# New charges for five kinds of elementwise work in a build-time plan, and a new table that steers it

## The chip, the core and the metric

The kernel runs on one core of one Trainium2 chip. The metric is the device time of one launch in microseconds (us); the time before is 1015.88 us, the median of three runs (1014.32 to 1016.97). A core has five engines that run side by side, each with its own queue of instructions: TensorE (PE in the profile, with its weight loads as PEld) multiplies matrices into eight banks of PSUM; VectorE (DVE), ScalarE (ACT) and GpSimd (POOL) do elementwise work; SyncE (SP) issues the transfers, which sixteen DMA engines carry out. An instruction that needs another engine's result waits for it at the head of its own queue, and everything behind it waits too.

## The reference

Two attention blocks, A and B, read the same x (2048 tokens of 640 numbers) with their own weights, and a gate per token mixes their outputs. One block projects x to q, k and v, splits them into 32 heads of 20 and the tokens into 4 segments of 512. For each segment and head it takes causal softmax attention inside the segment and reads a memory M, z that holds the segments before:

```python
logits = einsum("bhqd,bhkd->bhqk", qs, ks) * scale + mask
a_dot  = einsum("bhqk,bhkd->bhqd", softmax(logits), vs)
pq  = phi(qs)                      # t + 1 where t > 0, else exp(t)
a_mem = einsum("bhld,bhde->bhle", pq, M) / (einsum("bhld,bhd->bhl", pq, z) + 1e-6)
o   = g * a_mem + (1.0 - g) * a_dot     # g = sigmoid(beta), one per head
M, z = M + phi(ks)^T vs, z + sum(phi(ks))
```

The block's output is o times wo, and the kernel's is `gate * a + (1 - gate) * b` with `gate = sigmoid(x . gate_w)`.

## The kernel before

The work is cut into eight rows t = 0 to 7: row t is block t % 2 in segment t // 2. A row has jobs for TensorE (projections of q, k, v and, one row later, of the output; 128 rows of the result at a time) and eight quads, each of four heads, so 64 quads in all. A quad i has ten score units (five S, which give the row maxima, and five T, which give the transposed scores for the exponentials) and one unit of attention times v. Between them stand smaller units: transposes, reads of the memory (`mem_unit`) and its updates. Products are made of three terms, since each operand is split into a high part (the rounded copy) and a low part (what rounding left). Most matmuls use half of the array's rows, and two such run side by side.

The order on every queue is written out when the kernel is built. The build runs a plan: a clock, a queue per engine (A, D, G, S for ScalarE, VectorE, GpSimd and SyncE) and a charge in microseconds for every piece of work. `put` (line 200) queues a piece with its charge and adds the charge to the engine's load; when the plan's engine is free, the piece of the best priority is written out, and what depends on it follows after the charge. TensorE's instructions are written out as the plan's clock moves on (`step`, line 1649). So the charges decide when the plan believes that an operand is there, and with it what TensorE's queue holds at that place. They don't delay anything on the chip. Three places choose an engine by load: `anyof` (line 217) takes the one whose load and charge are least in sum, `either` does it for ScalarE and VectorE, and `hi_lo_phi` (line 720) takes one of two ways through the feature map phi.

A table, `RULES`, steers the plan slot by slot (66 slots; one quad's S and T units fall in each; a slot without a row keeps the settings of the one before). `rules` (line 1690) reads eight settings: the order of the S and T units; `span`, the share of the slot over which they are spread; `calm`, the load on VectorE above which units of low priority, the memory's among them, are held back; `lag`, the time between the two halves of a product; `room`, the free buffers that T units need; `hold`, how much earlier a slot begins; `wait` and `wait2`, how long small units are held before they are taken.

The lines of the change lie in the weighing of a row's dots. For rows 0 to 6 the attention's sums go to DRAM (`send_dot`) and come back rearranged. When all eight quads of a row are there, `reciprocals` (line 1377) multiplies the denominators by the gates (line 1379, VectorE) and inverts them in two halves (line 1384). `mix` (line 1404) then handles five tiles of 128x512: the product with the inverse (line 1429 on VectorE or line 1430 on GpSimd), from row 2 on the transposed memory part added by VectorE (line 1496), the high part by ScalarE (line 1420), and the low part (line 1422 on VectorE or line 1423 on GpSimd). The output job of the row waits for them. GpSimd also makes the low parts of weights (line 543) and of x (line 590), and it masks the exponentials (line 1292). VectorE makes the row maxima (line 1196), and with three instructions it closes a memory unit (lines 897, 899 and 900).

Of the kernel before, what the change touches and what calls it, by code (L numbers as in the profile page):

```python
# [16 lines left out]
ALU = mybir.AluOpType  # L17

P = 128
D = 640  # L20
S = 2048
# [3 lines left out]
L = 512  # L25
KT = D // P
NB = L // P
# [10 lines left out]
def r32(ap):  # L38
    return ap.bitcast(F32)
# [3 lines left out]
def tile_gated_mix_infini_attn(  # L43
# [17 lines left out]
    nc = tc.nc  # L61
# [27 lines left out]

    RULES = {  # L90
# [60 lines left out]
    }  # L151
    rule = {}
    DONE = {"A": 0.27, "D": 0.26, "G": 0.22, "S": 0.0}
    FULL, LEADT = 0.113, 0.056
# [45 lines left out]
    def put(e, dur, emit, then=None, prio=5):  # L200
        heapq.heappush(ready[e], (prio, next(seq), dur, emit, then))
        load[e] += dur
        start_next(e)
# [1172 lines left out]

    def reciprocals(t, d, g):
        def gates():
            put("D", 0.9, lambda: nc.vector.scalar_tensor_tensor(
                out=r32(d), in0=r32(d), scalar=gcol[t % 2], in1=r32(g), op0=ALU.mult, op1=ALU.mult), lambda: half(0), prio=2)  # L1380

        def half(c):
            cols = slice(L // 2 * c, L // 2 * (c + 1))
            put("D", 1.78, lambda: nc.vector.reciprocal(r32(d[:, cols]), r32(d[:, cols])),
                (lambda: half(1)) if c == 0 else done, prio=2)
            if c == 0:
                big.give(g)

        def done():
            inverse[t] = d  # L1390
            for fn in waiting.pop(t, []):
                fn()

        landed = then_all(2, gates)
        b = t % 2
        dma(0.8, lambda: nc.sync.dma_start(
            out=r32(d), in_=lanes_of(t)[:, DH:DH + 1, :].to_broadcast([H, 4, L])), landed, prio=-1, lat=1.2)
        dma(0.8, lambda: nc.sync.dma_start(
            out=r32(g), in_=rowg[t // 2][NB * b:NB * b + NB, :].rearrange("n p -> (n p)")[None, :].to_broadcast([P, L])), landed, prio=-1, lat=1.2)
# [4 lines left out]
    def mix(t, k, y):  # L1404
# [14 lines left out]
        def two_parts(hi, lo):  # L1419
            put("A", 0.515, lambda: nc.scalar.copy(hi, r32(y)), lambda: anyof(  # L1420
                2, lambda: (big.give(y), OTs.__setitem__((t, k), (hi, lo))),
                D=(0.85, lambda: nc.vector.tensor_tensor(out=lo, in0=r32(y), in1=r32(hi), op=ALU.subtract)),  # L1422
                G=(1.25, lambda: nc.gpsimd.tensor_tensor(out=lo, in0=r32(y), in1=r32(hi), op=ALU.subtract))), prio=2)

        def weigh():
            r = inverse[t]
            anyof(
                2, weighed,
                D=(0.9, lambda: nc.vector.tensor_tensor(out=r32(y), in0=r32(y), in1=r32(r), op=ALU.mult)),  # L1429
                G=(1.4, lambda: nc.gpsimd.tensor_tensor(out=r32(y), in0=r32(y), in1=r32(r), op=ALU.mult)))  # L1430

        def landed():
            if t in inverse:
# [358 lines left out]
```

## Time and profile before

| | |
|---|---|
| median of three runs | 1015.88 us (1014.32 to 1016.97) |
| profiled execution, its own time | 1016.54 us |
| its span, first to last instruction | 1014.8 us |
| mean granted TensorE clock | 0.995 of full speed |
| busy: TensorE, weight loads | 1002.1 us (99%), 855.5 us (84%) |
| busy: VectorE, ScalarE, GpSimd | 769.3 us (76%), 659.5 us (65%), 612.3 us (60%) |

The page gives busy time per engine. A table of stretches gives the same per window: first the window, then its length, then busy time and number of instructions for TensorE, its weight loads, VectorE, ScalarE and GpSimd, then the granted clock, the share of the DMA engines in use and GB/s. A group's row gives line, engine, operation, what it writes and reads, the shapes and the count, then busy us and mean ns of one, then the engine's idle time before such instructions and who ended it. A timeline's row gives start, length, engine, line and operation, and in brackets the idle time before it and who ended it; rows with a count of more than one are merged. The chain of waits follows the end back to the start; its rows give start, length and what it was.

### The profile page before, as it was taken

The page shows a single profiled execution, that of the slowest core. Times are in us where ns is not written, and L with a number is a line of the kernel's source. Part 1 is how long each engine was busy: PE and PEld are TensorE (multiplying, and loading weights), DVE is VectorE, ACT ScalarE, POOL GpSimd, SP SyncE. Part 2 cuts the span into 40 slices and gives each one's busy share as a digit, 9 for nine tenths or more (in the row PEclk, how much of TensorE's full clock was granted, in tenths as well). Part 3 has the DMA queues.
Part 4 walks back from the last instruction along what each step waited for, and adds up shares of the span by engine and source line. Part 5 has one row for each costly group of instructions (what it writes and reads, how often), then busy time and mean ns, then how long its engine had stood idle before and what let it go on. Part 6 is the DMA issues. An engine that isn't in the chain of part 4 may idle for free.

```text
span 1014.8 us, 30827 instructions
## 1 busy us (share of the span) xinstructions
PE 1002.1 (99%) x11260; PEld 855.5 (84%) x11260; DVE 769.3 (76%) x2604; ACT 659.5 (65%) x1341; POOL 612.3 (60%) x1040
## 2 busy tenths in 40 slices
PE   9999999999999999999999999999999999999998
PEld 7998888888888888878888878897889888878876
DVE  4688777976787778877578976888567897689764
ACT  5376776776566767757766666675676666675672
POOL 4465657676476655775646656486675656567571
PEclk9999999999999999999999999998999999999999
DMA  7999989898896988866768687795876979688531
GB/s 248 308 306 270 298 255 305 274 283 259 262 286 185 286 237 245 268 183 219 237 177 300 188 267 234 206 301 175 252 230 182 313 213 281 206 228 267 151 93 62
DMA packets 148886, 241.99 MB, mean 238 GB/s; under 512 B 13216, under 2 KB 46144, under 8 KB 148416
## 3 DMA queue, kind: packets, MB, share of 16 engines
q1 hardware_dynamic: 148736, 240.03, 77.2%
q8 instruction: 89, 1.46, 0.6%
q14 instruction: 61, 0.50, 0.2%
HBM read 150.83 MB, written 94.65 MB: 242 GB/s over the span
## 4 chain that ended last, share of the span: by engine, by line
PE 84%; DMA 6%; DVE 5%; ACT 1%; POOL 1%; issue 1%; SPq 1%; ACTq 0%; DVEq 0%; POOLq 0%
PE bank L773 50%; PE bank L1319 13%; PE bank L1299 7%; PE bank L1209 7%; PE bank L883 3%; PE bank L965 3%; PE bank L925 2%; DMA row<-dots 1%; DMA dots<-row 1%; DMA kd<-row 1%; DVE bank L1196 1%; PE bank L1234 1%; DVE row L1429 1%; DVE row L1422 1%; DMA row<-in_xT_dram 1%
## 5 line engine op out<-in xcount | busy, mean ns | idle before, releaser
L1196 DVE CUSTOM_DVE_ANT_0 bank<-bank,tri 128x256 f32<-128x256 f32 (+3 forms) x1024 | 474.7, 520 | 150.2 <-PE bank L1209 96.8
L773 PE MATMUL bank<-row,wh 64*128 64x512 f32 x2308 | 498.6, 403 | 0.6 <-DVE mw L897 0.6
L1291 ACT ACTIVATE p<-bank 128x512 f32<-128x512 f32 x588 | 324.0, 601 | 140.0 <-PE bank L1299 108.4
L1292 POOL TENSOR_SCALAR_AFFINE_SELECT p<-p 128x256 f32<-128x256 f32 (+1 forms) x588 | 219.2, 380 | 228.6 <-ACT p L1291 219.2
L773 PEld LDWEIGHTS bank<-row,wh 64*128 64x128 f32 x2308 | 319.8, 186 | 11.8 <-issue 1.1
L773 PE MATMUL bank<-row,wl 64*128 64x512 f32 x1154 | 293.3, 402 | 0.0
L543 POOL TENSOR_TENSOR wl<-wst,wh 128x640 fp32r<-128x640 f32 x115 | 181.3, 1581 | 58.1 <-ACT wh L541 51.7
L1209 PE MATMUL bank<-kst,qst 60*128 60x384 f32 (+3 forms) x1024 | 184.0, 317 | 1.8 <-DVE row L1349 0.8
L773 PEld LDWEIGHTS bank<-row,wl 64*128 64x128 f32 x1154 | 173.6, 186 | 5.0 <-issue 0.6
L1299 PE MATMUL bank<-qst,kst 62*128 62x128 f32 (+3 forms) x1024 | 176.4, 317 | 1.0 <-ACT vst L1015 0.5
L773 PE MATMUL bank<-wvh,row 64*128 64x320 f32 x1280 | 176.7, 312 | 0.0
L1319 PE MATMUL bank<-p,vst 128*32 128x384 f32 (+3 forms) x1936 | 148.9, 431 | 0.0
L773 PEld LDWEIGHTS bank<-wvh,row 64*128 64x128 f32 x1280 | 147.4, 185 | 1.0 <-issue 0.2
L1196 DVE DVE_READ_ACCUMULATOR2_ANT mx<- 128x1 f32 x1024 | 144.6, 141 | 0.0
L1209 PEld LDWEIGHTS bank<-kst,qst 60*128 60x128 f32 x1024 | 137.5, 186 | 8.2 <-DVE row L1349 1.2
L1299 PEld LDWEIGHTS bank<-qst,kst 62*128 62x128 f32 x1024 | 130.5, 186 | 7.3 <-DVE mx L1196 1.0
L1319 PEld LDWEIGHTS bank<-p,vst 128*32 128x32 f32 x1936 | 59.3, 110 | 87.4 <-issue 62.7
L541 ACT CAST wh<-wst 128x640 fp32r<-128x640 f32 x119 | 86.4, 741 | 20.2 <-PE bank L773 14.4
L773 PE MATMUL bank<-wvl,row 64*128 64x320 f32 x640 | 99.3, 310 | 0.0
L1349 ACT COPY row<-bank 128x512 f32<-128x512 f32 x61 | 36.0, 590 | 79.4 <-PE bank L1319 71.1
L773 PEld LDWEIGHTS bank<-wvl,row 64*128 64x128 f32 x640 | 80.0, 185 | 0.6 <-issue 0.4
L518 POOL TENSOR_TENSOR wvl<-wst,wvh 128x640 fp32r<-128x640 f32 (+1 forms) x48 | 64.0, 1338 | 17.3 <-ACT wvh L515 17.3
(117 smaller groups left out, 1213.5 us busy)
## 6 DMA issues: line engine op xcount, KB each, us to landing
qst<-qd SPq DMA_DIRECT2D x128, 240.0 KB
kst<-kd SPq DMA_DIRECT2D x128, 240.0 KB
qd<-row SPq DMA_DIRECT2D x40, 512.0 KB
kd<-row SPq DMA_DIRECT2D x40, 512.0 KB
dots<-row SPq DMA_DIRECT2D x56, 256.0 KB
wst<-wmix SPq DMA_DIRECT2D x35, 320.0 KB
row<-dots SPq DMA_DIRECT2D x42, 256.0 KB
qd<-row SPq DMA_DIRECT2D x40, 256.0 KB
```

What stands on the lines that cost most here:

```text
L518: put("G", 0.77 * n, lambda: nc.gpsimd.tensor_tensor(out=wl[:, a:b, :], in0=w3, in1=r32(wh[:, a:b, :]), op=ALU.subtract), end, prio=4)
L541: put("A", 0.625, lambda: nc.scalar.copy(wh, w3), lambda: put(lo_eng, lo_cost, lambda: lo.tensor_tensor(out=wl, in0=w3, in1=r32(wh), op=AL ...
L543: lambda: lo.tensor_tensor(out=wl, in0=w3, in1=r32(wh), op=ALU.subtract), end, prio=3), prio=6)
L773: return nc.tensor.matmul(bank_of, lhsT=w[ROWS[half]], rhs=x_[ROWS[half]], start=start, stop=stop)
L883: return nc.tensor.matmul(pm[:, a - h0:c - h0, :].rearrange("p h e -> p (h e)"), lhsT=r32(pqTs[t, m][ROWS[half], P * n:P * (n + 1)]), rhs= ...
L1196: put("D", w / 960.0 + 0.105, lambda: nc.vector.tensor_tensor_reduce(out=sc[:, off:off + w], in0=sc[:, off:off + w], in1=tri[:, L - w:], s ...
L1209: lane_ops[half].append((mm(w), lambda pair=pair, qb=qb, off=off, w=w, r=r, sc=sc: nc.tensor.matmul(sc[:, off:off + w], lhsT=q[r, pair, P ...
L1291: put("A", 0.483, lambda: nc.scalar.activation(pt, sc, AF.Exp, scale=SCALE), lambda: (bank.give(sc), put("G", 0.15 + 0.105 * len(todo), la ...
L1292: "G", 0.15 + 0.105 * len(todo), lambda: nc.gpsimd.affine_select(out=blocks, in_=blocks, pattern=[[0, len(todo)], [1, P]], base=0, channel ...
L1299: lane_ops[half].append((mm(w), lambda pair=pair, kb=kb, off=off, w=w, r=r, sc=sc: nc.tensor.matmul(sc[:, off:off + w], lhsT=k[r, pair, P ...
L1319: nc.tensor.matmul(po[32 * j:32 * j + 32, P * kb:], lhsT=vst[t % 2][:, kb, h * E1:h * E1 + 32], rhs=pts[i, n, f][0][:, off:off + w], start ...
L1349: either(0.483, lambda: nc.scalar.copy(r32(oT), po), 0.605, lambda: nc.vector.tensor_copy(r32(oT), po), end, 2)
```

## The change

Five charges change: the gate 0.90 to 1.00, a product on VectorE 0.90 to 1.05 and on GpSimd 1.40 to 1.50, a low part on VectorE 0.85 to 0.95 and on GpSimd 1.25 to 1.35. The table is replaced: row 0 stays, 57 other rows take the place of 59. Counting what a slot without a row inherits, 63 of 66 slots have other settings than before.

```diff
     RULES = {
         0: "TSTSTSTSTS 0.933 2.38 0.30 4 0.0 3.08 1",
-        1: "TSTSTSTSTS 1.010 2.38 0.27 8 0.0 1.6 1.60",
-        2: "TSTSTSTSTS 1.036 2.04 0.30 6 0.0 1.6 0.40",
-        3: "STSTSTSTST 0.976 2.38 0.30 8 0.1 1.6 1",
-        4: "TSTSTSTSTS 1.010 1.52 0.31 8 1.9 1.31 1.66",
...
+        1: "TSTTSSTSTS 0.988 3.22 0.30 4 0.0 1.6 1",
+        2: "STSTSTSTST 0.986 2.38 0.37 8 0.0 1.6 1",
+        3: "TSTSTSTSTS 1.010 1.76 0.35 4 3.4 1.6 1",
+        4: "TSTSTSTSTS 1.029 3.65 0.29 8 0.0 1.6 1",
...
     def reciprocals(t, d, g):
         def gates():
-            put("D", 0.9, lambda: nc.vector.scalar_tensor_tensor(
+            put("D", 1.0, lambda: nc.vector.scalar_tensor_tensor(
...
         def two_parts(hi, lo):
             put("A", 0.515, lambda: nc.scalar.copy(hi, r32(y)), lambda: anyof(
                 2, lambda: (big.give(y), OTs.__setitem__((t, k), (hi, lo))),
-                D=(0.85, lambda: nc.vector.tensor_tensor(out=lo, in0=r32(y), in1=r32(hi), op=ALU.subtract)),
-                G=(1.25, lambda: nc.gpsimd.tensor_tensor(out=lo, in0=r32(y), in1=r32(hi), op=ALU.subtract))), prio=2)
+                D=(0.95, lambda: nc.vector.tensor_tensor(out=lo, in0=r32(y), in1=r32(hi), op=ALU.subtract)),
+                G=(1.35, lambda: nc.gpsimd.tensor_tensor(out=lo, in0=r32(y), in1=r32(hi), op=ALU.subtract))), prio=2)
...
             anyof(
                 2, weighed,
-                D=(0.9, lambda: nc.vector.tensor_tensor(out=r32(y), in0=r32(y), in1=r32(r), op=ALU.mult)),
-                G=(1.4, lambda: nc.gpsimd.tensor_tensor(out=r32(y), in0=r32(y), in1=r32(r), op=ALU.mult)))
+                D=(1.05, lambda: nc.vector.tensor_tensor(out=r32(y), in0=r32(y), in1=r32(r), op=ALU.mult)),
+                G=(1.5, lambda: nc.gpsimd.tensor_tensor(out=r32(y), in0=r32(y), in1=r32(r), op=ALU.mult)))
```

108 rows, old and new, of the table RULES are left out of this document.

## The prediction

> **What bounds the kernel now.** I read the page first, then the table of stretches, then TensorE's timeline around every gap, then the groups of the repriced lines.
>
> ```profile
> span 1014.8 us, 30827 instructions
> PE 1002.1 (99%) x11260; PEld 855.5 (84%) x11260; DVE 769.3 (76%) x2604; ACT 659.5 (65%) x1341; POOL 612.3 (60%) x1040
> ```
>
> TensorE sets the time: 12.7 us of the span are left without a matmul, and some of that is the head and the tail, which the change doesn't touch. In 25 us stretches, these are the inner ones with a visible loss (left out: four that lose under 0.1 us each):
>
> ```profile
> core 0: us, PE busy (x) PEld busy (x) DVE busy (x) ACT busy (x) POOL busy (x), PEclk, DMA share, GB/s
> ...
> 150.00:175.00 25.00, 24.52 (x294) 20.69 (x292) 17.94 (x47) 16.69 (x36) 18.60 (x29) 1.00 0.97 292
> ...
> 300.00:325.00 25.00, 24.23 (x274) 20.26 (x272) 18.92 (x62) 16.02 (x32) 18.87 (x30) 1.00 0.65 193
> ...
> 400.00:425.00 25.00, 24.51 (x301) 21.11 (x293) 21.07 (x57) 16.20 (x34) 17.60 (x28) 1.00 0.90 289
> 425.00:450.00 25.00, 23.35 (x257) 20.32 (x255) 21.25 (x78) 15.45 (x31) 18.40 (x26) 0.93 0.57 174
> ...
> 575.00:600.00 25.00, 24.20 (x270) 21.08 (x268) 20.34 (x74) 15.10 (x31) 14.07 (x33) 1.00 0.86 270
> ...
> 675.00:700.00 25.00, 24.21 (x272) 19.68 (x270) 22.25 (x58) 17.08 (x36) 18.48 (x23) 0.86 0.79 236
> ...
> 925.00:950.00 25.00, 24.49 (x307) 21.35 (x305) 22.42 (x82) 15.66 (x33) 15.94 (x28) 1.00 0.56 165
> ```
>
> Idle in them: 0.48 + 0.77 + 0.49 + 1.65 + 0.80 + 0.79 + 0.51 = 5.49 us. Two also show a lower granted clock: 25 x (1 - 0.93) = 1.75 us and 25 x (1 - 0.86) = 3.50 us, together 5.25 us of lost beats, about as much as the gaps. A new order can win back at most some 10.7 us. The gaps themselves, on TensorE's timeline:
>
> ```profile
> 302.04 0.49 PE L773 MATMUL bank<-row,wh 64*128 64x512 f32 x1 [0.60 <-DVE mw L897]
> 305.98 0.38 PE L1209 MATMUL bank<-kst,qst 60*128 60x256 f32 x1 [0.17 <-DVE O L900]
> 687.72 0.80 PE L1209 MATMUL bank<-kst,qst 60*128 60x512 f32 x2 [0.31 <-DVE row L1496]
> 688.87 0.93 PE L883 MATMUL bank<-mbd,row 64*128 64x84 f32 x3 [0.35 <-ACT p L1291]
> 925.54 0.50 PE L1299 MATMUL bank<-qst,kst 62*128 62x384 f32 x4 [0.33 <-DVE row L729]
> ```
>
> ```profile
> 172.11 0.50 PE L1299 MATMUL bank<-qst,kst 62*128 62x512 f32 x1 [0.48 <-ACT vst L1015]
> 420.91 0.49 PE L1209 MATMUL bank<-kst,qst 60*128 60x512 f32 x1 [0.49 <-ACT row L1349]
> 436.98 0.23 PE L1234 MATMUL bank<-ident,mt 64*32 64x64 f32 x1 [1.59 <-POOL mt L1221]
> 592.18 0.50 PE L1209 MATMUL bank<-kst,qst 60*128 60x384 f32 x4 [0.80 <-DVE row L1349]
> ```
>
> The first fence of gaps (1.76 us) lies where a row's dots are weighed and split, behind VectorE. Its timeline there, with one undisturbed product for comparison:
>
> ```profile
> 185.17 0.69 DVE L1429 TENSOR_TENSOR row<-row,row 128x512 f32<-128x512 f32 x1
> 299.93 1.79 DVE L1422 TENSOR_TENSOR row<-row,row 128x512 fp32r<-128x512 f32 x1
> 302.67 2.44 DVE L1422 TENSOR_TENSOR row<-row,row 128x512 fp32r<-128x512 f32 x2
> 685.14 1.92 DVE L1429 TENSOR_TENSOR row<-row,row 128x512 f32<-128x512 f32 x1
> 919.84 2.86 DVE L1429 TENSOR_TENSOR row<-row,row 128x512 f32<-128x512 f32 x2
> ```
>
> The slow product at 685.14 ran beside this on GpSimd:
>
> ```profile
> 684.98 1.54 POOL L543 TENSOR_TENSOR wl<-wst,wh 128x640 fp32r<-128x640 f32 x1 [0.17 <-ACT wh L541]
> ```
>
> The second fence of gaps (3.36 us) has another cause. ScalarE takes its instructions in their written order and stood behind a transfer:
>
> ```profile
> 170.14 0.62 ACT L586 CAST row<-row 128x512 fp32r<-128x512 f32 x1 [1.19 <-DMA row<-in_xT_dram]
> 417.77 0.62 ACT L586 CAST row<-row 128x512 fp32r<-128x512 f32 x1 [0.68 <-DMA qst<-qd]
> 435.91 0.62 ACT L586 CAST row<-row 128x512 fp32r<-128x512 f32 x1 [2.16 <-DMA row<-in_xT_dram]
> 590.87 0.60 ACT L732 ACTIVATE row<-bank 128x512 f32<-128x512 f32 x1 [2.29 <-DMA kd<-row]
> ```
>
> No edited price bears on these four.
>
> **The change, part by part.** It takes no product, copy or transfer away; it alters charges in the plan and the table that steers it, and so the order on every queue and, where the plan chooses by load, the engine.
>
> ```profile
> L1430 POOL TENSOR_TENSOR row<-row,row 128x512 f32<-128x512 f32 x23 | 31.9, 1406 | 7.1 <-DVE row L1384 5.2 <-DVE fw L1468 1.9
> L1423 POOL TENSOR_TENSOR row<-row,row 128x512 fp32r<-128x512 f32 x19 | 26.5, 1400 | 10.4 <-ACT row L1420 9.7 <-ACT mr L1251 0.6
> L1422 DVE TENSOR_TENSOR row<-row,row 128x512 fp32r<-128x512 f32 x16 | 18.2, 1148 | 0.0
> L1429 DVE TENSOR_TENSOR row<-row,row 128x512 f32<-128x512 f32 x12 | 15.3, 1291 | 0.0
> L1379 DVE SCALAR_TENSOR_TENSOR row<-row,gcol,row 128x512 f32<-128x512 f32 x7 | 7.4, 1053 | 6.7 <-DMA row<-rowg 5.4 <-DMA kst<-kd 1.3
> ```
>
> Prices against means: VectorE's product 0.90 to 1.05 (measured 1.291), its low part 0.85 to 0.95 (1.148), the gate 0.90 to 1.00 (1.053); GpSimd's product 1.40 to 1.50 (1.406), its low part 1.25 to 1.35 (1.400). The undercharge on VectorE was 12 x 0.391 + 16 x 0.298 + 7 x 0.153 = 10.5 us over seven stretches and becomes 12 x 0.241 + 16 x 0.198 + 7 x 0.053 = 6.4 us, so four tenths of the error go. GpSimd goes from 2.9 us short to 23 x 0.094 - 19 x 0.05 = 1.2 us over. The division between the engines should hardly move: for a product the difference of the two prices goes from 0.50 to 0.45, for a low part it stays 0.40. The third choice by load, which of two ways the feature map takes, can shift a pass or two from VectorE to ScalarE:
>
> ```profile
> L722 DVE TENSOR_SCALAR bank<-bank 128x512 f32<-128x512 f32 x35 | 24.3, 701 | 0.0
> L732 ACT ACTIVATE row<-bank 128x512 f32<-128x512 f32 x25 | 15.3, 614 | 3.0 <-DMA kd<-row 2.3 <-DVE row L1422 0.7
> ```
>
> Now 35 tiles go by VectorE and 25 by ScalarE; one more by ScalarE takes 0.70 us off VectorE, and I cost it at nothing, because ScalarE is busy 65% of the span and covers it. Without that cover it would be 0.61 us of ScalarE's time each.
>
> What that buys, gap by gap, is the rise of the charges on the chain just ahead, since the plan then places the waiting matmul that much later and puts other matmuls in front. Before 302.04 stand a product and a low part (0.15 + 0.10 = 0.25 of 0.60). Before 305.98 two low parts (0.20, so all 0.17). Before 687.72 one product (0.15 of 0.31), which the chain of waits shows directly:
>
> ```profile
> 685.28 1.79 DVE row L1429
> 687.07 0.61 DVE row L1496
> ```
>
> I give the 0.35 at 688.87 nothing, since it follows the same delay. Before 925.54 two products (0.30 of 0.33). Sum: 0.25 + 0.17 + 0.15 + 0.30 = 0.87 us. If the table alone decides what stands there, this is 0; if all five gaps go, 1.76.
>
> The larger term is the clock behind 687.72, which stood at half for most of seven microseconds:
>
> ```profile
> 688.00:689.00 1.00, 0.65 (x3) 0.14 (x3) 1.00 (x4) 0.82 (x2) 0.69 (x2) 0.50 0.87 188
> ```
>
> That episode is the 3.50 us of the 675:700 row. I take all of it as won, with ends of 0 and 3.50: longer gaps (0.60 at 302.04, 0.80 at 592.18) dropped no clock, so this needs an unlucky coincidence of a gap with a thin run of short matmuls, and a rewritten stretch will seldom repeat it. [...]
>
> The table gives 63 of the 66 slots other settings (order of score units, spread, load limit, lag, early start, delays), counting what a missing row inherits. No row of the trace prices this. Its ends are one episode like 425:450 lost or gained, 1.65 + 1.75 = 3.40 us each way, and I take the middle, 0: the same transfers, with the same charges in the plan, will be late somewhere. SP's queue is reordered with the rest, so a transfer such as the one of x at 435.91 can as well come earlier as later; who is queued behind a late one is ScalarE's copies, and TensorE behind those. Waits of one half of the array while the other works don't show as idle; they lie in these ends too.
>
> Sum: 1016.54 (the profiled execution: span 1014.8 and 1.74 around it) - 0.87 - 3.50 = 1012.17. That execution lies 0.66 over the median 1015.88 of the runs shown, so the forecast is **1011.5 us**.
>
> **The rivals.** *No change, 1015.0 us.* The crowded stretches keep their stalls, because a flat charge is wrong there both ways: the same product takes 0.69 and 1.92 us, and 0.87 on 1.92 is not covered by 1.05. Only the 0.87 us of gaps go, a half-clock episode comes back somewhere: 1016.54 - 0.87 - 0.66. For it: the new charges are still under the means on VectorE. Against: half-clock episodes number only two in 1,015 us. [...]
>
> *Slower, 1019.3 us.* The load limit ("calm", mostly 2.38 us) holds memory units back while VectorE's queue is charged above it. Three products now add 0.45 us to that queue, so memory units start later, the updates that wait for them too, and with them the values' job of the next row, until TensorE has no unit to fill with. The price is that of the nearest row, 425:450: 1.65 us of gap and 1.75 us of clock, 1015.88 + 3.40. It decides once a memory unit is held longer than the jobs planned between it and the values' job last. For it: VectorE is busy 22.25 of 25 us at 675:700. Against: TensorE waited for a memory bank's reader in only 0.60 + 0.17 us here.
>
> *Much faster, 1005.1 us.* The new order also covers the late transfers: all 5.49 + 5.25 us go, 1015.88 - 10.74 = 1005.1. Against: nothing in the plan's charge for a transfer changes.
>
> **How the numbers follow.** A measurement of this kernel tells 0.3%, 3.05 us, from no change: faster is under 1012.8, slower over 1018.9. Chances: my forecast 0.42 (own range 1008 to 1015), no change 0.23, slower 0.23, much faster 0.12. Faster: 0.32 of my case, 0.12 of the last, 0.01 of no change, 0.45. Same: 0.10 of my case and 0.20 of no change, 0.30. Slower: 0.23 and 0.02 of no change, 0.25. The range reaches from the last case to the slower one with half a further episode (1.75) on it: 1004.5 to 1021.
>
> **What would show it.** Right: VectorE's products and low parts still near 1.2 us each, a 25 us table with at most one stretch of reduced clock, idle in the weighing stretches down to about 1 us, and gaps behind transfers of some 3 us in other places. Wrong: two or more stretches under 0.95 of the clock, or gaps behind the weighing as long as 1.76 us in sum. The forecast fails if the clock episode is not chance but belongs to the weighing, or if the new table moves a late transfer in front of ScalarE's copies more often than four times.

## The result and the profile after

The changed kernel takes 1022.10 us (median of five runs, 1020.31 to 1023.17) where the kernel before, on the same chip, takes 1015.03 us (five runs, 1012.20 to 1016.97). The ratio is 1.007 with an interval of 1.0055 to 1.0085: the change makes the kernel 0.7% slower. The forecast was 1011.5 us in a range of 1004.5 to 1021, so both the sign and the range were wrong.

Lines behind the table stand two lower in the changed kernel: the product of the projections is L771 (it was L773), the weighing's product on VectorE L1427 (L1429), its low part L1420 (L1422). The first lines of the page after:

```profile
span 1020.4 us, 30866 instructions
PE 1005.0 (98%) x11260; PEld 860.1 (84%) x11260; DVE 767.3 (75%) x2592; ACT 665.9 (65%) x1355; POOL 609.7 (60%) x1038
```

The span grew by 5.6 us. TensorE's idle part grew from 12.7 to 1020.4 - 1005.0 = 15.4 us, which is 2.7. The other 2.9 us are *busy* time, 1002.1 to 1005.0, although TensorE runs the same 11260 matmuls, and one by one they lasted as long as before (in the mean 357 ns before, 356 after). Its costliest groups after, with the count, then busy time and the mean ns of one:

```profile
L771 PE MATMUL bank<-row,wh 64*128 64x512 f32 x2308 | 507.5, 404 | 0.0
L771 PE MATMUL bank<-row,wl 64*128 64x512 f32 x1154 | 302.9, 402 | 0.0
L771 PE MATMUL bank<-wvh,row 64*128 64x320 f32 x1280 | 182.3, 314 | 1.7 <-ACT vst L1013 1.7
L771 PE MATMUL bank<-wvl,row 64*128 64x320 f32 x640 | 103.2, 312 | 0.0
```

And the same four of the kernel before:

```profile
L773 PE MATMUL bank<-row,wh 64*128 64x512 f32 x2308 | 498.6, 403 | 0.6 <-DVE mw L897 0.6
L773 PE MATMUL bank<-row,wl 64*128 64x512 f32 x1154 | 293.3, 402 | 0.0
L773 PE MATMUL bank<-wvh,row 64*128 64x320 f32 x1280 | 176.7, 312 | 0.0
L773 PE MATMUL bank<-wvl,row 64*128 64x320 f32 x640 | 99.3, 310 | 0.0
```

Busy time of a group is the time in which at least one of its matmuls runs. The second group has the same 1154 matmuls of 402 ns, but covers 302.9 us and not 293.3. These matmuls use half of the array's rows; a longer cover at equal count and equal length means that fewer of a group run side by side. For one group that can also mean that another group runs beside it more often (the covers of different groups overlap, so their growths can't be added), so I counted all records of the two traces: for 326.5 us before and 344.8 us after, one to three matmuls are in flight (begun and not ended); for 675.5 and 660.2 us, four or more. So fewer run side by side. That one half of the array then works alone is my reading; the records don't name the half. No gap shows it, and TensorE counts as busy.

The granted clock improved. These are the inner 25 us stretches in which the kernel after loses most (nine more lose under 0.5 us each); after the window and its length stand the busy times of TensorE, weight loads, VectorE, ScalarE and GpSimd, then the granted clock, the DMA share and GB/s:

```profile
175.00:200.00 25.00, 24.47 (x252) 20.95 (x250) 23.21 (x68) 18.11 (x37) 16.53 (x26) 1.00 0.82 268
300.00:325.00 25.00, 24.36 (x272) 21.30 (x271) 21.54 (x68) 15.89 (x32) 17.15 (x21) 1.00 0.70 202
375.00:400.00 25.00, 24.10 (x303) 21.38 (x301) 19.04 (x74) 15.11 (x33) 9.23 (x20) 1.00 0.65 200
600.00:625.00 25.00, 24.38 (x239) 19.46 (x237) 18.40 (x70) 14.83 (x32) 15.29 (x26) 1.00 0.75 228
675.00:700.00 25.00, 23.81 (x288) 21.84 (x290) 18.65 (x54) 16.82 (x35) 14.60 (x20) 1.00 0.80 260
800.00:825.00 25.00, 23.88 (x304) 21.47 (x301) 21.64 (x51) 14.95 (x32) 17.05 (x22) 1.00 0.89 259
900.00:925.00 25.00, 23.29 (x237) 18.82 (x235) 19.27 (x56) 16.65 (x35) 13.72 (x25) 0.98 0.81 253
925.00:950.00 25.00, 24.75 (x317) 22.74 (x315) 19.46 (x67) 14.07 (x29) 17.50 (x22) 0.95 0.66 192
```

Lost beats in the inner stretches are now 25 x 0.02 + 25 x 0.05 = 1.75 us against 5.25 before. Those 3.5 us lie inside the busy time. Without them the busy time would be 1002.1 - 5.25 = 996.9 before and 1005.0 - 1.75 = 1003.3 after: about 6.4 us more, a remainder, which I put down to matmuls that run less side by side. That is the main item.

The gaps have the same two causes as before. On TensorE's timeline after, these are the four gaps behind a transfer (at 378, 604, 676 and 922) and three of the nine behind VectorE at the weighing (at 186, 305 and 812; the other six are 0.23 to 0.38 us each):

```profile
186.34 0.51 PE L1207 MATMUL bank<-kst,qst 60*128 60x384 f32 x4 [0.22 <-DVE mx L1194]
304.74 0.38 PE L1207 MATMUL bank<-kst,qst 60*128 60x256 f32 x1 [0.37 <-DVE mx L1194]
378.31 0.50 PE L1207 MATMUL bank<-kst,qst 60*128 60x256 f32 x3 [0.90 <-DVE mx L1194]
604.28 0.50 PE L1297 MATMUL bank<-qst,kst 62*128 62x384 f32 x4 [0.62 <-DVE row L1070]
676.19 0.56 PE L771 MATMUL bank<-wvh,row 64*128 64x320 f32 x4 [1.67 <-ACT vst L1013]
811.92 0.44 PE L1297 MATMUL bank<-qst,kst 62*128 62x384 f32 x2 [0.72 <-DVE mx L1194]
922.22 0.50 PE L1207 MATMUL bank<-kst,qst 60*128 60x256 f32 x2 [1.61 <-ACT p L1289]
```

The transfers' rows sum to 0.90 + 0.62 + 1.67 + 1.61 = 4.80 us, against 3.36 before. For the two longest, ScalarE's timeline shows the copy that stood waiting for data, with x at 672 and a weight at 921:

```profile
672.46 1.34 ACT L584 CAST row<-row 128x512 fp32r<-128x512 f32 x2 [1.62 <-DMA row<-in_xT_dram]
921.22 0.46 ACT L513 CAST wvh<-wst 128x320 fp32r<-128x320 f32 x1 [2.03 <-DMA wst<-in_b_wv_dram]
```

The weighing's gaps sum to 3.1 us against 1.76 before, and its instructions on VectorE still take far longer than the raised charges (1.05, 0.95, 1.00):

```profile
L1420 DVE TENSOR_TENSOR row<-row,row 128x512 fp32r<-128x512 f32 x17 | 18.5, 1113 | 0.0
L1427 DVE TENSOR_TENSOR row<-row,row 128x512 f32<-128x512 f32 x13 | 15.8, 1237 | 2.3 <-DMA row<-dots 1.3 <-POOL p L1290 0.9
L720 DVE TENSOR_SCALAR bank<-bank 128x512 f32<-128x512 f32 x21 | 14.6, 704 | 0.0
L1377 DVE SCALAR_TENSOR_TENSOR row<-row,gcol,row 128x512 f32<-128x512 f32 x7 | 8.0, 1143 | 7.5 <-DMA row<-rowg 7.5
```

The third row is the feature map: 21 tiles go by VectorE where 35 did, so the choice by load moved 14, not one or two.

### The profile page after: what moved, and what is told of

Read it like the earlier page. It is cut to its first block, busy times and chain, and to the rows that moved or that the text cites. A ratio compares the mean times of both kernels' runs of the same rounds, so it can differ in the third digit from the quotient of the medians.

```text
span 1020.4 us, 30866 instructions
## 1 busy us (share of the span) xinstructions
PE 1005.0 (98%) x11260; PEld 860.1 (84%) x11260; DVE 767.3 (75%) x2592; ACT 665.9 (65%) x1355; POOL 609.7 (60%) x1038
## 4 chain that ended last, share of the span: by engine, by line
PE 84%; DMA 7%; DVE 4%; issue 2%; ACT 1%; SPq 1%; POOL 0%; DVEq 0%; ACTq 0%
PE bank L771 49%; PE bank L1317 13%; PE bank L1297 7%; PE bank L1207 7%; PE bank L881 3%; PE bank L963 3%; PE bank L923 2%; DMA row<-dots 1%; DVE bank L1194 1%; DMA dots<-row 1%; PE bank L1232 1%; DVE row L1427 1%; DMA wst<-in_b_wv_dram 1%; DMA row<-in_xT_dram 1%; DMA qd<-row 1%
## 5 line engine op out<-in xcount | busy, mean ns | idle before, releaser
L1194 DVE CUSTOM_DVE_ANT_0 bank<-bank,tri 128x384 f32<-128x384 f32 (+3 forms) x1024 | 474.3, 520 | 147.0 <-PE bank L1207 110.5
L771 PE MATMUL bank<-row,wh 64*128 64x512 f32 x2308 | 507.5, 404 | 0.0
L1289 ACT ACTIVATE p<-bank 128x512 f32<-128x512 f32 x580 | 318.5, 599 | 138.3 <-PE bank L1297 108.5
L771 PEld LDWEIGHTS bank<-row,wh 64*128 64x128 f32 x2308 | 324.3, 186 | 8.7 <-issue 1.0
L771 PE MATMUL bank<-row,wl 64*128 64x512 f32 x1154 | 302.9, 402 | 0.0
L771 PE MATMUL bank<-wvh,row 64*128 64x320 f32 x1280 | 182.3, 314 | 1.7 <-ACT vst L1013 1.7
L1207 PE MATMUL bank<-kst,qst 60*128 60x128 f32 (+3 forms) x1024 | 180.1, 316 | 3.5 <-ACT p L1289 1.6
L771 PEld LDWEIGHTS bank<-row,wl 64*128 64x128 f32 x1154 | 177.4, 186 | 4.3 <-issue 0.6
L1297 PE MATMUL bank<-qst,kst 62*128 62x384 f32 (+3 forms) x1024 | 176.4, 316 | 2.3 <-DVE mx L1194 1.3
L771 PEld LDWEIGHTS bank<-wvh,row 64*128 64x128 f32 x1280 | 151.0, 185 | 3.8 <-ACT vst L1013 1.9
L1317 PE MATMUL bank<-p,vst 128*32 128x256 f32 (+3 forms) x1908 | 145.7, 428 | 0.0
L1207 PEld LDWEIGHTS bank<-kst,qst 60*128 60x128 f32 x1024 | 132.1, 186 | 11.0 <-ACT p L1289 2.8
L771 PE MATMUL bank<-wvl,row 64*128 64x320 f32 x640 | 103.2, 312 | 0.0
L771 PEld LDWEIGHTS bank<-wvl,row 64*128 64x128 f32 x640 | 82.6, 185 | 0.0
```

What stands on the lines that cost most here:

```text
L771: return nc.tensor.matmul(bank_of, lhsT=w[ROWS[half]], rhs=x_[ROWS[half]], start=start, stop=stop)
L1194: put("D", w / 960.0 + 0.105, lambda: nc.vector.tensor_tensor_reduce(out=sc[:, off:off + w], in0=sc[:, off:off + w], in1=tri[:, L - w:], s ...
L1207: lane_ops[half].append((mm(w), lambda pair=pair, qb=qb, off=off, w=w, r=r, sc=sc: nc.tensor.matmul(sc[:, off:off + w], lhsT=q[r, pair, P ...
L1289: put("A", 0.483, lambda: nc.scalar.activation(pt, sc, AF.Exp, scale=SCALE), lambda: (bank.give(sc), put("G", 0.15 + 0.105 * len(todo), la ...
L1297: lane_ops[half].append((mm(w), lambda pair=pair, kb=kb, off=off, w=w, r=r, sc=sc: nc.tensor.matmul(sc[:, off:off + w], lhsT=k[r, pair, P ...
L1317: nc.tensor.matmul(po[32 * j:32 * j + 32, P * kb:], lhsT=vst[t % 2][:, kb, h * E1:h * E1 + 32], rhs=pts[i, n, f][0][:, off:off + w], start ...
```

## The experiments

The numbers are medians; ratios are to the kernel before on the same chip.

**1 to 4: the parts alone, and both charges under a plain table.** The first keeps the old table and raises the charges, the second takes the new table with the old charges. In the third and fourth the table has one row for all slots, with the old and with the new charges.

```diff
 # prices only: table of before; table only: table of after
-                D=(0.9, lambda: nc.vector.tensor_tensor(out=r32(y), ...
+                D=(1.05, lambda: nc.vector.tensor_tensor(out=r32(y), ...
 # (and the other four charges)
 # the two plain ones:
     RULES = {
-        0: "TSTSTSTSTS 0.933 2.38 0.30 4 0.0 3.08 1",
...
+        0: "TSTSTSTSTS 1.010 2.38 0.30 8 0.0 1.6 1",
     }
```

> The five new charges with the old table. Theory A (table and charges are one fit: the rows answer to the plan's own times, so either half alone throws the order off): far slower than both kernels, above 1030 us, with idle and half-idle TensorE spread over many stretches. Theory B (the new charges are right and shift the order in the right places, the loss of 7 us comes from the new table): 1010 to 1016 us. Theory C (the new charges do the harm): near the changed kernel, 1019 to 1025 us.

> The new table with the old charges. Theory A (one fit): above 1030 us, as with the charges alone. Theory B (the table does the harm): near the changed kernel, 1019 to 1025 us. Theory C (the charges do the harm, the table is as good as the old one): 1010 to 1018 us.

> A table of one row (the settings that most rows of both tables share) with the old charges: neither set of charges has rows fitted to it. Theory A: some tens of us slower than before, 1035 to 1060 us. Theory B and C: a table's rows are worth little, within 10 us of before, 1015 to 1025 us.

> The same one-row table with the new charges, so the charges alone differ from the run before it. Theory B (charges nearer the measured means place TensorE's waits better): 2 us or more faster than with the old charges. Theory C: 2 us or more slower. Theory A with redraw (any change of a charge deals the order anew): a difference of either sign, and gaps in the weighing stretches no shorter in sum.

The charges alone: 1065.78 us, 1.0475 (1.0430 to 1.0521). The table alone: 1070.73 us, 1.0530 (1.0492 to 1.0567). The plain table: 1060.34 us with the old charges, 1.0433 (1.0407 to 1.0459), and 1055.11 with the new ones, 1.0383 (1.0357 to 1.0410). Each half of the change costs about 5%, and together they cost 0.7%. So a table and its charges are one fit: a fitted table that meets other charges is no better than a table that was never fitted (1.0433 and 1.0383). Whether the plan itself ends later in these four is not on record. Under the plain table the new charges are 5 us faster, which is no more than equal tables differ by in experiments 9 to 12. This page, of the charges alone, shows where the 5% are:

```profile
span 1062.9 us, 30808 instructions
PE 1043.9 (98%) x11260; PEld 882.9 (83%) x11260; DVE 765.2 (72%) x2602; ACT 661.3 (62%) x1346; POOL 607.9 (57%) x1037
```

It is 48.1 us longer than before, and TensorE still counts as 98% busy: its idle part grew only from 12.7 to 19.0 us, its busy time by 41.8. (The table alone: a span of 1068.6 us, of which TensorE is busy 1049.7 and idle 18.9.) A lower granted clock explains a part of that. This is the span of the charges alone with its mean clock:

```profile
core 0: 1062.9 us, clock 0.987
```

Against 0.995 before that makes 1062.9 x 0.013 - 1014.8 x 0.005 = 8.7 us. Some 33 us are left. An order that costs 5% hides most of it in "busy".

**5 and 6: the weighing made light.** In both kernels VectorE's product and low part are replaced by a fill of the same tile, which reads nothing; the order stays.

```diff
-                D=(0.85, lambda: nc.vector.tensor_tensor(out=lo, in0=r32(y), in1=r32(hi), op=ALU.subtract)),
+                D=(0.85, lambda: nc.vector.memset(r32(lo), 0.0)),
-                D=(0.9, lambda: nc.vector.tensor_tensor(out=r32(y), in0=r32(y), in1=r32(r), op=ALU.mult)),
+                D=(0.9, lambda: nc.vector.memset(r32(y), 0.001)),
```

> The kernel before in its own order; VectorE's 12 products and 16 low parts of the weighing are replaced by constant fills of the same tiles (one output, no input), so the weighing by the inverse and the low part are left out there. Theory W (what these cost over their charges makes the weighing gaps): the gaps at 302.04, 305.98, 687.72, 688.87 and 925.54 (1.76 us) and the half clock behind 687.72 (3.50 us) go: 1010 to 1012.5 us. Rival L (late transfers and the order itself set the time): within 1.5 us of the kernel before, a new gap takes the place of the old ones.

> The same fills in the changed kernel, in its own order. Theory W: the gaps behind VectorE in its weighing stretches (0.22, 0.31, 0.37, 0.26, 0.38, 0.35, 0.72, 0.40 and 0.23 us, 3.2 us in sum) go, 1017.5 to 1019.5 us. Rival L: 1020.5 to 1023 us, since its two large gaps (1.67 at 676.19, 1.61 at 922.22) lie behind transfers.

Before with fills: 1009.93 us, 0.9955 (0.9943 to 0.9967). After with fills: 1016.10 us, 1.0018 (1.0008 to 1.0029), better than was expected. Their pages:

```profile
span 1006.7 us, 30821 instructions
PE 996.1 (99%) x11260; PEld 855.1 (85%) x11260; DVE 754.0 (75%) x2604; ACT 658.8 (65%) x1341; POOL 600.3 (60%) x1040
```

```profile
span 1015.4 us, 30858 instructions
PE 1002.9 (99%) x11260; PEld 859.8 (85%) x11260; DVE 749.1 (74%) x2592; ACT 666.5 (66%) x1355; POOL 598.5 (59%) x1038
```

The weighing's instructions on VectorE cost some 5 us over the fills in either order (1014.86 to 1009.93 before; after, the ratio falls from 1.0070 to 1.0018): more than the 1.76 us of gaps that I read in the profile. The 5 us are not the slowness alone: a fill takes 0.49 us where even an undisturbed product takes 0.69 (185.17), it also relieves GpSimd (612.3 to 600.3 us of busy time before), and in the first profile the half clock at 675:700 is gone. But the two kernels still lie 6.2 us apart without it, nearly as far as with it (7.1). So VectorE's part of the weighing is not what makes the changed kernel slower.

**7 and 8: the copies of x later in ScalarE's queue.** The copies of x for segment 0 stay. The later ones are still ScalarE's, but they are written out together with the low part on GpSimd, so that ScalarE's queue meets them later.

```diff
-            put("A", 0.515, lambda: nc.scalar.copy(hi, r32(st)), low, prio=6)
+            put("A", 0.515, lambda: nc.scalar.copy(hi, r32(st)) if s == 0 else None, low, prio=6)
 # low, for s > 0: the copy is issued together with the low part
+            put("G", 1.25, both, ...)
```

> The kernel before with its charges; ScalarE's high parts of x for segments 1 to 3 (15 instructions of line 586) are written out right ahead of GpSimd's low part instead of a charge earlier, so ScalarE's queue meets them later. Theory X (x lands late at the head of ScalarE's queue): the gaps at 172.11, 420.91 and 436.98 (2.56 us) and the half clock behind the last (1.75 us) go, 1011 to 1013 us. Rival: the wait moves to GpSimd, whose masks and row maxima stand behind the low part: 1014 to 1018 us.

> The same move in the changed kernel. Theory X: the gap of 1.67 us at 676.19 goes, with what one half of the array waited around it: 1018.5 to 1020.5 us. Rival: 1021 to 1024 us, the wait moves to GpSimd.

Before: 1015.45 us, 1.0006 (0.9997 to 1.0014), no gain. After: 1020.05 us, 1.0055 (1.0041 to 1.0069), an interval that overlaps that of the change itself. The largest gaps that were aimed at went, and others came. The kernel before with this edit has these two, among others (its line numbers are six higher):

```profile
350.06 0.21 PE L1240 MATMUL bank<-ident,mt 64*32 64x64 f32 x1 [0.93 <-ACT p L1297]
687.73 0.50 PE L1215 MATMUL bank<-kst,qst 60*128 60x512 f32 x2 [0.31 <-DVE row L1502]
```

The 1.59 us at 436.98 and its clock drop are gone; the two smaller ones only shrank (0.48 to 0.23 and 0.49 to 0.32 us), 0.93 us at 350.06 is new, and 687.73 is as it was. In the changed kernel the 1.67 us at 676 are gone, 0.74 at 417.92 is new, and 1.30 at 921.09 stays. Here a late wait moved to the next place. In the kernel before, the rival's range holds; in the changed kernel Theory X's does, with 2 us that can't be told from nothing.

**9 to 12: other tables for the same charges.** Is it these charges, or this table? Settings of many slots were redrawn at random, and a redraw was kept where the build's plan ends as early as with the table that it came from: two with the old charges, two with the new.

```diff
 # first redraw with the old charges; all 66 slots have a row, from before's settings
-        1: "TSTSTSTSTS 1.010 2.38 0.27 8 0.0 1.6 1.60",
-        2: "TSTSTSTSTS 1.036 2.04 0.30 6 0.0 1.6 0.40",
+        1: "TSTSTSTSTS 1.039 3.36 0.29 6 2.1 2.48 1.68",
+        2: "TSTSTSTSTS 0.948 3.84 0.34 6 1.0 0.36 0.40",
...
```

> Old charges; the old table changed at random in many rows, keeping those changes after which the plan still ends within 2 us of the old plan; the order differs from 90 us on. Theory P (the new charges cost the 7 us): like the kernel before, 1013 to 1017 us. Theory R (any new fit of the table deals the order anew, and the time scatters by several us around a mean that the old kernel happens to lie below): 1015 to 1023 us.

> The same with other random changes; the order differs from 30 us on. Theory P: 1013 to 1017 us. Theory R: 1015 to 1023 us, and not the same as the first.

> New charges; the new table changed at random in many rows in the same way, the plan ending within 1 us of the changed kernel's; the order differs from 64 us on. Theory P: like the changed kernel, 1020 to 1025 us. Theory R: 1015 to 1024 us. Theory T (this one table was unlucky, the charges help): 1010 to 1016 us.

> The same with other random changes. Theory P: 1020 to 1025 us. Theory R: 1015 to 1024 us. Theory T: 1010 to 1016 us.

Old charges: 1016.73 us, 1.0026 (1.0014 to 1.0037), and 1019.25, 1.0049 (1.0034 to 1.0064). New charges: 1019.66 us, 1.0052 (1.0037 to 1.0067), and 1022.13, 1.0083 (1.0065 to 1.0101). With the two originals that is 1.000, 1.0026, 1.0049 on the one side and 1.0052, 1.0070, 1.0083 on the other. Three tables of one set of charges, which the plan holds for about equal, lie up to 0.5% apart on the chip, and 0.7% is little more than that spread. The two sets touch but don't mix, which three against three do by chance one time in ten. So most of the loss can be the luck of one fit; whether the charges themselves add a few tenths of a per cent can't be told from three tables each, and stays open. None of the three with the new charges beats the kernel before.

**13 and 14: GpSimd's instructions in two halves.** At 685.14 VectorE's product took 1.92 us beside GpSimd's work. Here three kinds of GpSimd's long two-input instructions (the weighing's product and low part, and the weights' low part at line 543) are written as two, each over about half of the columns; its low parts of x and of the v weights stay whole. The charges and so the order stay.

```diff
+def halves(eng, out, in0, in1, op):
+    c = out.shape[1] // 2
+    for s in (slice(0, c), slice(c, None)):
+        eng.tensor_tensor(out=out[:, s], in0=in0[:, s], in1=in1[:, s], op=op)
...
-                G=(1.25, lambda: nc.gpsimd.tensor_tensor(out=lo, in0=r32(y), in1=r32(hi), op=ALU.subtract))), prio=2)
+                G=(1.25, lambda: halves(nc.gpsimd, lo, r32(y), r32(hi), ALU.subtract))), prio=2)
...
-                G=(1.4, lambda: nc.gpsimd.tensor_tensor(out=r32(y), in0=r32(y), in1=r32(r), op=ALU.mult)))
+                G=(1.4, lambda: halves(nc.gpsimd, r32(y), r32(y), r32(r), ALU.mult)))
 # and the same for the weights' low part
```

> The kernel before; each of GpSimd's products and low parts of the weighing, and each of its low parts of weights (lines 1430, 1423 and 543), is written as two instructions of about half the width; charges and order stay. Theory B (VectorE's two-input instruction stands behind a whole GpSimd instruction): VectorE's products and low parts fall from means of 1.29 and 1.15 us to about 1.0 us, the weighing gaps shrink, 1011 to 1014 us. Rival: the cost of a second instruction (some 0.1 us for each of 157) fills GpSimd, masks come later, 1015 to 1020 us.

> The same in the changed kernel. Theory B: 1017 to 1020.5 us. Rival: 1021.5 us or more.

Before: 1012.86 us, 0.9988 (0.9966 to 1.0010); the runs lie from 1009.37 to 1021.24 us, and no difference can be told. After: 1018.72 us, 1.0058 (1.0035 to 1.0080), which overlaps with the change as it was. The durations tell more than the times. In the kernel before with the halves (the low part is its L1428, the product its L1435):

```profile
L1428 DVE TENSOR_TENSOR row<-row,row 128x512 fp32r<-128x512 f32 x16 | 14.9, 938 | 0.2 <-ACT row L1426 0.2
L1435 DVE TENSOR_TENSOR row<-row,row 128x512 f32<-128x512 f32 x12 | 10.9, 929 | 0.5 <-DMA row<-dots 0.5
```

The same instructions at the same places fell from 1148 to 938 and from 1291 to 929 ns.

**15 and 16: VectorE half empty.** On top of the fills, the row maxima run over 64 columns, which takes some 250 us of work off VectorE.

```diff
-                        out=sc[:, off:off + w], in0=sc[:, off:off + w], in1=tri[:, L - w:],
+                        out=sc[:, off:off + 64], in0=sc[:, off:off + 64], in1=tri[:, L - w:L - w + 64],
```

> The kernel before with the constant fills of the weighing, and with each row maximum taken over 64 columns instead of 128 to 512, which leaves most of each maximum out: VectorE loses some 200 us of work, in the same order. Theory S (the order itself, transfers and pairing): 1006 to 1010 us, and the changed kernel with the same edit stands 4 us or more above it. Theory V (VectorE late in many places): 1004 to 1008 us, and the two are within 2 us.

> The same in the changed kernel's order. Theory S: 1011 to 1015 us, 4 us or more above the other. Theory V: 1004 to 1009 us, within 2 us of it.

Before: 1006.22 us, 0.9925 (0.9912 to 0.9938). After: 1013.29 us, 0.9989 (0.9978 to 1.0000). Their pages:

```profile
span 1006.9 us, 30834 instructions
PE 997.2 (99%) x11260; PEld 856.7 (85%) x11260; DVE 504.6 (50%) x2604; ACT 657.3 (65%) x1341; POOL 601.8 (60%) x1040
```

```profile
span 1011.9 us, 30877 instructions
PE 999.3 (99%) x11260; PEld 859.0 (85%) x11260; DVE 498.6 (49%) x2592; ACT 665.3 (66%) x1355; POOL 598.6 (59%) x1038
```

With VectorE busy half of the time, the two medians are still 7.1 us apart (the two profiled executions 5.0). So the difference does not come from VectorE's load, in the weighing or elsewhere. What runs side by side still differs: one to three matmuls are in flight for 322.0 us in the first trace and for 337.1 in the second. What is left is the order as written: which matmuls stand beside each other, and which copies stand behind which transfers. That is reached by exclusion. ScalarE and GpSimd were not lightened in the same way, and no run changed the pairing of matmuls alone.

**17 and 18: the halves told apart.** One splits only the weighing's 42 instructions on GpSimd, the other only the weights' 115 low parts, both in the kernel before; the edits are those of 13, each alone.

> The kernel before; only GpSimd's products and low parts of the weighing (42 instructions) are split in two. If these block VectorE: its products and low parts stay near the 0.93 us that both splits gave, at a third of the added work on GpSimd: 1010.5 to 1013 us. If the weights' low parts do: means near 1.15 us and 1013 to 1016 us.

> The kernel before; only GpSimd's low parts of weights (115 instructions) are split in two. If these block VectorE: means near 0.95 us, 1011 to 1014 us. If the weighing's own do: means near 1.15 us, 1014 to 1018 us.

The weighing alone: 1012.55 us (1011.95 to 1012.92) against 1014.87 on the same chip, 0.9974 (0.9964 to 0.9984). That beats both kernels. The weights alone: 1013.25 us, 0.9981 (0.9970 to 0.9993). VectorE's two groups and the split product on GpSimd in the first:

```profile
L1428 DVE TENSOR_TENSOR row<-row,row 128x512 fp32r<-128x512 f32 x16 | 14.3, 899 | 0.3 <-ACT row L1426 0.3
L1435 DVE TENSOR_TENSOR row<-row,row 128x512 f32<-128x512 f32 x12 | 11.1, 946 | 0.0
...
L45 POOL TENSOR_TENSOR row<-row,row 128x256 f32<-128x256 f32 x46 | 37.8, 847 | 5.1 <-DVE row L1390 2.2 <-issue 1.5 <-DVE fw L1474 1.1
```

And in the second:

```profile
L1428 DVE TENSOR_TENSOR row<-row,row 128x512 fp32r<-128x512 f32 x16 | 18.3, 1151 | 0.0
L1435 DVE TENSOR_TENSOR row<-row,row 128x512 f32<-128x512 f32 x12 | 14.6, 1239 | 0.3 <-DMA row<-dots 0.3
```

So what stretches most of VectorE's products and low parts is the weighing's own work on GpSimd: splitting it takes 28 instructions from some 1.2 us to 0.92 in the mean, although GpSimd itself pays (a product of 1406 ns becomes two of 847). The weights' split leaves those two means nearly as they were (1151 and 1239). But it is not the weighing's work alone. The product that the prediction quotes, 1.92 us at 685.14, ran beside a weights' low part. With the weighing split it is as slow as before, beside the same low part:

```profile
681.25 1.93 DVE L1435 TENSOR_TENSOR row<-row,row 128x512 f32<-128x512 f32 x1
681.09 1.54 POOL L549 TENSOR_TENSOR wl<-wst,wh 128x640 fp32r<-128x640 f32 x1 [0.17 <-ACT wh L547]
```

With the weights split it is short:

```profile
681.89 1.12 DVE L1435 TENSOR_TENSOR row<-row,row 128x512 f32<-128x512 f32 x1
```

And the stretch around it then reads:

```profile
675.00:700.00 25.00, 24.03 (x252) 19.03 (x254) 22.14 (x67) 14.53 (x30) 17.38 (x24) 0.86 0.69 209
```

The gap of 0.31 us that stood at 687.72 is gone there (the one after it is 0.78 us and not 0.35), and the clock is at 0.86 as before. What either split gains in time is not explained: 17 shortens VectorE's instructions and gains 0.26%, 18 hardly does and gains 0.19%, and the intervals overlap.

## Why the prediction was wrong

**TensorE sets the time: right. "A new order can win back at most some 10.7 us": too narrow a measure.** That bound counted gaps and lost beats, which is all that an order *shows*; no run won more than that, but an order can lose far more. Experiments 1 to 4 lost 3.8 to 5.3%, and in the first two of them the idle part of the span grew by only 6 us, to 19.0 and 18.9. The time in which one half of the array works alone was named in the prediction in one sentence, but it got no size of its own.

**The table at 0 with ends of 3.40 us: this is the step that failed.** I took the nearest row with a visible loss as the measure of what 63 changed slots can do. Measured from the two profiled executions, the new order cost 6.4 us of hidden time and 1.4 us more behind transfers (4.80 against 3.36), 7.8 us where I had put 0 and at most 3.40. (The order comes from table and charges together; experiments 1 and 2 show that the two can't be priced apart.) The redraws give the size that I lacked: tables of one and the same set of charges lie up to 0.5%, about 5 us, apart.

**The charges, -0.87 us: not borne out.** Gaps at the weighing went from 1.76 to 3.1 us, past the 1.76 that the prediction named as a sign of being wrong. How much of that the charges did and how much the table can't be told, since the charges alone made another order altogether (1065.78 us). The charges came nearer to the means and the means hardly moved (1.291 to 1.237, 1.148 to 1.113, the gate 1.053 to 1.143), but the single instruction varies more than the correction. The product on VectorE after the change, twice within five microseconds:

```profile
809.78 1.42 DVE L1427 TENSOR_TENSOR row<-row,row 128x512 f32<-128x512 f32 x1
...
814.47 0.69 DVE L1427 TENSOR_TENSOR row<-row,row 128x512 f32<-128x512 f32 x1 [1.08 <-DMA row<-dots]
```

And on GpSimd beside the first:

```profile
809.36 1.29 POOL L1428 TENSOR_TENSOR row<-row,row 128x512 f32<-128x512 f32 x1 [0.84 <-DVE row L1382]
```

The slow product ends 0.55 us after GpSimd's, and the 0.72 us gap at 811.92 follows it. A charge of 1.05 fits neither. That the slow one is held up by GpSimd's instruction fits experiments 13 and 17: with GpSimd's instruction cut in two, VectorE's product fell from a mean of 1.29 us to 0.93 and 0.95. In the weighing the prediction also read too little: its gaps were 1.76 us, but with fills in place of VectorE's part the kernel is 4.9 us faster (in the profile of experiment 5 the piece of half clock at 675:700 is gone as well).

**The clock, -3.50 us: right in size by luck, wrong in reason.** The loss went from 5.25 to 1.75 us, but not as forecast: both old episodes went with the old order, and a new one came at 900 to 950. The reason that I gave, that the episode hangs on the 0.31 us gap at 687.72 and that a small thing would undo it, does not hold: in experiment 18 that gap is gone and the episode is not. That it takes a gap together with a thin run of short matmuls was my guess, and no run shows it. Among the experiments with the order of the kernel before, the 675:700 stretch had its clock of 0.86 again in 7, 13, 15, 17 and 18, and was free of it in 5 alone.

**The choice by load: right in direction, wrong in number.** 14 tiles moved to ScalarE, whose busy time grew by 6.4 us; it is still busy only 65% of the span. Its cost alone was not tried.

**Late transfers: right in kind.** "Some 3 us in other places" became 4.80 us in other places, all of them with a copy of ScalarE's or an instruction of VectorE's standing behind a transfer.

**The sum** against the profiled executions: weighing +1.4 (forecast -0.87), transfers +1.4 (0), clock -3.5 (-3.50), hidden +6.4 (0), together +5.7 us, and the span grew by 5.6. Two figures of the prediction are slightly off and change nothing: GpSimd's undercharge before is 23 x 0.006 + 19 x 0.15 = 3.0 us and not 2.9, and the last case gives 1005.1 us as the range's lower end, where 1004.5 stands.

**The rivals.** The slower one came nearest in time (1019.3) and is not what happened: none of the gaps after the change that are shown stands behind a reader of a memory's bank (the copy of v at 676 was late because ScalarE stood behind x before it), and its price came from gaps and clock, while most of the loss is neither. The rival of no change had the right premise, that a flat charge is wrong both ways, but took the table for neutral as well.

## What to carry to other kernels

When an order is fitted to a plan's charges, a correction of the charges comes with a new fit, and the new fit's luck (here up to 0.5%, 5 us, between tables that the plan holds for equal) is larger than the 0.87 us that I credited to the charges: cost the fit with that spread, not with the nearest gap. Where halves of the array ran side by side here, busy time was not useful time (with the charges alone the span grew by 48.1 us, 41.8 of them busy); at equal count and equal mean, compare busy time less the beats lost to the clock, and how many matmuls are in flight. If one engine's instruction takes 0.69 us at one time and 1.9 at another, look for the other engine's instruction that runs beside it, before repricing: cutting that one in two shortened the product here, though what that alone is worth in time is not shown.

## What the runs showed of the hardware

In the kernel before, VectorE's products and low parts of 128x512 took 0.68 to 0.91 us where they began while no product or low part ran on GpSimd (8 of the 28), and 0.74 to 1.92 where they began inside one (20): 0.69 us at 185.17, 1.79 at 299.93 beside GpSimd's products of 128x512, and 1.92 at 685.14 beside a weights' low part of 128x640. With GpSimd's instructions in two halves the means fell from 1.291 and 1.148 us to 0.929 and 0.938 (experiment 13). In experiment 17 the halves cost 42 more instructions and 6 us more of GpSimd's time (612.3 to 618.5, some 0.15 us each), and the kernel was 0.26% faster; experiment 18 gained 0.19% with these means nearly as they were (1.239 and 1.151), so the gain can't be put down to the shorter durations. I had taken the long durations for a fixed condition to be priced.

Away from the ends of the two profiles the lower clock came three times, at 0.50 each time: before for 3.4 us from 438.4 (in windows of 1 us from 438 it reads 0.70, 0.50, 0.50, 0.59) and for 6.8 us from 687.6, after for 3.4 us from 924.0, over the border of two stretches. The rows of 25 us put the losses at 1.75, 3.50 and 1.75 us. What starts a piece stays open. Experiments 5 and 15 have the same fills in the same order, and only the second shows the 0.86:

```profile
675.00:700.00 25.00, 24.00 (x258) 18.74 (x258) 14.45 (x77) 14.12 (x28) 15.48 (x24) 0.86 0.60 181
```

The gaps next to the three drops are 1.59 us, up to 436.98, and 0.31 us, up to 687.72, before, and 1.61 us, up to 922.22, after. The second drop began inside its gap, the others 1.4 and 1.8 us behind theirs. The 1.67 us up to 676.19 after the change are longer than all three, and the clock stayed at 1.00 behind them (675:700).
